# A list scheduler that interleaves two transformer layers: steps chosen by the tile mode of the matrix engine

## The chip, the cores and the metric

The kernel runs on one core of a Trainium2 chip. The core has five engines with an instruction queue each: PE (TensorE, matrix products; its weight loads are listed apart as PEld), ACT (ScalarE, functions such as exp), DVE (VectorE, elementwise and reductions), POOL (GpSimd) and SP (SyncE, here only the issue of DMAs). Products land in PSUM, which has eight banks of 128 x 512 f32. The metric is the device time of one execution in microseconds (us).

## The reference

The input x has 2048 rows of 512 values. Four layers follow each other, A, B, A, B, each adding its output to x after a layer norm; both A layers share their weights, and so do both B layers.

```python
def _A_ref(x, mem0, Wq, Wk, Wv, Wo, seg_len):        # seg_len 32, 8 memory rows, 32 heads of 128
    mem = mem0
    for s in range(n_seg):                            # 64 segments, one after the other
        h = concatenate([mem, x[segment s]])          # 40 rows
        q, k, v = h @ Wq, h @ Wk, h @ Wv              # per head
        p = softmax(where(mask, q @ k.T * scale, -1e9))
        o = (p @ v) @ Wo
        mem = o[:8]                                   # the next segment needs it
        outs.append(o[8:])

def _B_ref(x, wqkv, wo):                              # 32 heads of 16, full attention over 2048 rows
    q, k, v = x @ wqkv
    return softmax(q @ k.T * 0.25) @ v @ wo
```

An A layer is a chain of 64 segments, since each takes its eight memory rows from the one before. A B layer attends from every row to every row without a mask, so its last outputs need the last keys.

## The kernel before, in words

**A segment** is 22 steps on PE, each some 16 to 32 products: Q0 to Q3 and K0 to K3 (projections, `qk_group`, L472), S0 and S1 (scores of 16 heads each, `s_group`, L499, followed by exp on ACT, and mask, sum, reciprocal and scaling on DVE), V0 to V3 (values, `v_round`, L487), T0 and T1 (transposes of the probabilities, `pt_group`, L526), P0 and P1 (probabilities times values, `pv_group`, L538), W0 to W3 (output projection, `wo_part`, L550). The order in which they are considered is a string:

```python
PLAN = "Q0 K0 Q1 K1 S0 Q2 K2 Q3 K3 S1 T0 V0 V1 P0 V2 V3 T1 P1 W0 W1 W2 W3".split()
```

At its end the eight memory rows are copied into the next segment's input (L644).

**Tile modes.** PE can be used as one 128 x 128 array, or split into row or column strips that work side by side. Q, K, W, the B projections and all transposes of 128 x 128 use the whole array (`full`). S, T and V use two column halves of 64 (`col64`), P two row halves (`row64`), the scores of a B unit four row strips of 32 (`S` in the planner's books), the sums of a B unit four column strips of 32 (`PV`).

**A B layer** is cut into runs (one query chunk of up to 512 columns, one group of four heads, some key tiles) and each run into one to four units. A unit is 512 columns of key tile by query (one key tile by 512 queries, or four by 128): `emit_qk` (L388) writes the scores of four heads to three fixed PSUM banks (`b_SX`) and a fourth taken from a pool of four; ACT takes the exp of the three (L390) and then of the fourth (L391); later `pv_mm` (L401) multiplies the probabilities with the values and adds into the one bank `b_oacc`. The last unit of a run closes it: DVE copies the sum out (L706) or adds it to an earlier partial sum that came by DMA (L713), and the partial sum is stored, or, where the run is final, transposed and divided (`finish`, `tq`, L840); when all eight head groups of a tile are done, `out_tile` transposes (L872) and projects it (L881). There are 1040 units in all, 520 for each B layer. As tiles of 128 rows of an A layer become ready (every fourth segment), `tile_done` queues their projections as a chain of steps and adds runs: 32 units after the fourth tile of layer A, then 8, 24, 8, 56 after the next four, 16, 48, 16, 80, then 24, 72, 24, and 112 after the sixteenth. Runs are taken by layer and then by query chunk. The first B layer's units are worked during the first and second A layer, the second's during the second A layer and after it.

**The planner.** PE's order is written by a greedy loop in Python, `step`, that keeps a modelled clock of PE, ACT and DVE (`Clock`; a change of mode is counted with 0.11 us there). At each call it has four candidates with a modelled ready time each: A, the next step of the segment (`a_pick` looks at the first four open ones and takes the first that is ready); U, the scores of the next unit (ready when `b_SX`, a bank and its operands are free, and fewer than three units wait for their sum); V, the sums of up to two waiting units whose probabilities are ready; M, the next function of a chain (projections, `tq`, `out_tile`). Before, the order is: M if ready, V if two are ready or it must be done, U if the segment is behind its quota, A, then U, V, and else whatever is ready first. `quota` gives each segment a number of units: an eighth of the backlog rounded up, more where the second A layer waits for outputs of the first B layer, at most 12. `segment` (L604) loops `while left or done < quota`: it goes on after W3 until the quota is reached. `drain_until` calls `step` without A, between the two A layers and at the end.

The orders of ACT, DVE, POOL and SP follow the order in which this loop emits their instructions. The scratch pool `t` (two buffers of 128 x 512 bf16) holds normed rows, transposed outputs and the working tile of `check`, which tests that softmax sums are in range; the sums of the A layers lie in `smA`, with 16 slots of one segment each, and are tested every sixteenth segment.

## Time and profile before

| what | value |
|---|---|
| median of 2 runs | 3600.22 us (3599.82 to 3600.61) |
| the profiled execution | 3589.69 us |
| span of its instructions | 3587.9 us |
| mean granted clock of PE | 0.917 |
| PE busy (matrix products) | 3112.4 us, 87% |
| PEld busy (weight loads) | 2281.5 us, 64% |
| ACT busy | 2522.1 us, 70% |
| DVE busy | 1594.7 us, 44% |
| POOL busy | 369.9 us, 10% |

In the rows below, times are in us. A row of a timeline has the start, the length, the engine, the line of the kernel, the operation with its tiles, how many instructions are merged in it (`x32`), and in brackets the idle time of the engine just before it with what ended it. The ends of products on PE are modelled, so steps are timed from the start of one to the start of the next. Rows of windows have the window, its length, and busy time with the number of instructions of each engine; then the granted PE clock, the DMA share and GB/s.

### The profile page before, as it was taken

Reading aid. Unit: us, or ns where it says so; the run is one execution under the profiler, and the core shown is the slowest. Engines: PE = TensorE matmul, PEld = TensorE weight load, DVE = VectorE, ACT = ScalarE, POOL = GpSimd, SP = SyncE. Lnnn points to the kernel's source line nnn. Section 1 sums busy time; section 2 is a strip of 40 time slices with the busy share of each in tenths; the row PEclk is TensorE's granted clock in tenths of the full one; section 3 lists DMA queues with packets and bytes.
Section 4 is the critical chain, followed back from the end, with each engine's and each line's share of the span. In section 5 each row is a group of like instructions: output and inputs, shape, how many; then the busy total and the mean of one; then the engine's idle time right before and its main releaser. Section 6 shows DMA issues by size and latency. Waiting matters only on the chain.

```text
span 3587.9 us, 186067 instructions
## 1 busy us (share of the span) xinstructions
PE 3112.4 (87%) x85206; PEld 2281.5 (64%) x85249; DVE 1594.7 (44%) x3887; ACT 2522.1 (70%) x3367; POOL 369.9 (10%) x621
## 2 busy tenths in 40 slices
PE   4999999999998898788899999999998898877555
PEld 3887777776776765455677767777676675543332
DVE  1333434555545454355454544455564554434001
ACT  1444666767778788766876666676867778777886
POOL 0000001111111111101010001111111111000000
PEclk9999999999999998789999999999999999866555
DMA  6001112333334243434332122242334334343441
GB/s 219 16 20 34 38 46 75 98 91 99 112 98 127 82 141 100 122 106 129 97 91 64 42 65 68 78 117 80 112 104 121 109 92 146 101 123 117 122 115 43
DMA packets 318476, 337.25 MB, mean 94 GB/s; under 512 B 93296, under 2 KB 251120, under 8 KB 317680
## 3 DMA queue, kind: packets, MB, share of 16 engines
q1 hardware_dynamic: 279520, 221.67, 22.2%
q0 software_dynamic: 32384, 94.68, 8.2%
q8 instruction: 668, 10.94, 1.3%
q10 hardware_dynamic: 5776, 8.91, 0.8%
q14 instruction: 128, 1.05, 0.1%
HBM read 230.47 MB, written 94.63 MB: 91 GB/s over the span
## 4 chain that ended last, share of the span: by engine, by line
PE 73%; ACT 12%; issue 8%; DVE 4%; DMA 3%; SPq 0%; POOL 0%; ACTq 0%; DVEq 0%; POOLq 0%
PE bank L472 24%; PE bank L550 12%; PE bank L487 11%; ACT b_pt L390 10%; PE b_SX L388 10%; PE b_oacc L401 6%; PE bank L499 2%; PE bank L526 2%; PE bank L791 2%; PE bank L538 1%; DVE a_V L221 1%; PE bank L840 1%; PE bank L812 1%; DMA a_Wv<-in_A_Wv_dram 1%; ACT b_pt L391 1%
## 5 line engine op out<-in xcount | busy, mean ns | idle before, releaser
L390 ACT ACTIVATE b_pt<-b_SX 128x1536 bf16<-128x1536 f32 (+2 forms) x1040 | 1490.8, 1433 | 536.2 <-PE bank L388 487.8
L388 PE MATMUL b_SX<-b_q,b_k 32*128 32x128 bf16 (+1 forms) x6624 | 455.7, 292 | 281.7 <-ACT b_pt L390 269.7
L391 ACT ACTIVATE b_pt<-bank 128x512 bf16<-128x512 f32 (+2 forms) x1040 | 612.8, 589 | 0.5 <-PE bank L388 0.5
L472 PE MATMUL bank<-a_hT,a_Wq 128*128 128x40 bf16 x16384 | 509.7, 182 | 41.2 <-ACT a_QT L219 16.9
L487 PE MATMUL bank<-a_Wv,a_hT 128*64 128x512 bf16 x4096 | 509.7, 383 | 26.0 <-DVE a_V L221 15.6
L472 PEld LDWEIGHTS <-a_Wq 128*128 128x128 bf16 x16384 | 464.5, 97 | 95.3 <-issue 78.8
L472 PE MATMUL bank<-a_hT,a_Wk 128*128 128x40 bf16 x16384 | 506.7, 182 | 8.9 <-issue 4.8
L388 PEld LDWEIGHTS <-b_k 32*128 32x128 bf16 x8832 | 198.7, 99 | 464.2 <-issue 432.9
L550 PE MATMUL bank<-a_OT,a_Wo 128*128 128x40 bf16 x16384 | 475.7, 180 | 14.2 <-DVE a_OT L221 9.0
L472 PEld LDWEIGHTS <-a_Wk 128*128 128x128 bf16 x16384 | 459.7, 97 | 43.8 <-issue 36.4
L550 PEld LDWEIGHTS <-a_Wo 128*128 128x128 bf16 x16384 | 438.3, 96 | 58.0 <-issue 39.7
L401 PE MATMUL b_oacc<-b_pt,b_v 128*17 128x128 bf16 (+2 forms) x8832 | 440.0, 293 | 11.5 <-DVE b_ain L713 3.0
L388 PE MATMUL bank<-b_q,b_k 32*128 32x128 bf16 (+2 forms) x2208 | 445.9, 292 | 2.8 <-DVE b_xo L884 2.5
L487 PEld LDWEIGHTS <-a_hT 128*64 128x64 bf16 x4096 | 219.2, 110 | 195.5 <-issue 59.3
L504 DVE TENSOR_TENSOR a_pn<-a_pn,c_mask 128x256 bf16<-128x256 bf16 x256 | 74.6, 292 | 443.9 <-ACT a_pn L502 443.6
L401 PEld LDWEIGHTS <-b_v 128*17 128x17 bf16 x8832 | 155.3, 94 | 174.9 <-issue 139.6
L221 DVE CAST a_OT<-bank 128x320 bf16<-128x320 f32 x413 | 186.9, 485 | 132.9 <-PE bank L538 131.9
L713 DVE TENSOR_TENSOR b_ain<-b_oacc,b_ain 128x512 f32<-128x512 f32 (+2 forms) x256 | 167.7, 655 | 167.9 <-PE b_oacc L401 159.6
L221 DVE CAST a_QT<-bank 128x320 bf16<-128x320 f32 x259 | 126.8, 490 | 227.8 <-PE bank L472 223.8
L718 POOL DMA_DIRECT2D b_A<-b_aout x208 | 113.7, 547 | 1065.2 <-DVE b_aout L706 1037.0
L219 ACT CAST a_V<-bank 128x512 bf16<-128x512 f32 x292 | 168.9, 597 | 61.4 <-PE bank L487 57.9
L718 POOL DMA_DIRECT2D b_A<-b_ain x176 | 95.6, 543 | 952.8 <-DVE b_ain L713 927.3
(93 smaller groups left out, 2696.7 us busy)
## 6 DMA issues: line engine op xcount, KB each, us to landing
b_ain<-b_A SPq DMA_DIRECT2D x224, 256.0 KB, 2.8
b_A<-b_ain POOLq DMA_DIRECT2D x176, 256.0 KB, 2.6
b_k<-b_K SPq DMA_DIRECT2D x325, 128.0 KB, 2.4
b_q<-b_Q SPq DMA_DIRECT2D x240, 128.0 KB, 2.5
b_v<-b_V SPq DMA_DIRECT2D x448, 68.0 KB, 2.0
b_A<-b_aout POOLq DMA_DIRECT2D x192, 64.0 KB, 2.3
x_after_a<-a_xo POOLq DMA_DIRECT2D x32, 256.0 KB, 3.6
b_Q<-b_qst POOLq DMA_DIRECT2D x32, 256.0 KB, 3.6
```

What stands on the lines that cost most here:

```text
L219: self.nc.scalar.copy(dst, src)
L221: self.nc.vector.tensor_copy(dst, src)
L388: nc.tensor.matmul(out[t][:, j * qw:(j + 1) * qw], lhsT=k[32 * t:32 * t + 32, kj * 128:(kj + 1) * 128], rhs=q[32 * t:32 * t + 32, 0:qw], s ...
L390: nc.scalar.activation(pt[:, 0:3, 0:w], self.SX[:, 0:3, 0:w], ACT.Exp, scale=B_SCALE)
L391: nc.scalar.activation(pt[:, 3, 0:w], y.t[:, 0:w], ACT.Exp, scale=B_SCALE)
L401: self.nc.tensor.matmul(self.oacc[32 * t:32 * t + 17, 0:qw], lhsT=u.v[:, kj, 17 * t:17 * t + 17], rhs=u.p[:, t, j * qw:(j + 1) * qw], star ...
L472: nc.tensor.matmul(ps[:, u, :], lhsT=W[:, ft, h * DH:(h + 1) * DH], rhs=h_s[:, ft, 0:L], start=(n == 0) if ft_major else (ft == 0), stop=( ...
L487: nc.tensor.matmul(b.t[64 * ct:64 * ct + 64, :], lhsT=h_s[:, ft, :], rhs=self.Wv[:, ft, n * 512:(n + 1) * 512], start=(ft == 0), stop=(ft ...
L504: nc.vector.tensor_tensor(self.pn[:, st, :, 0:SEG], self.pn[:, st, :, 0:SEG], self.mask[:], ALU.mult)
L550: self.nc.tensor.matmul(ps[:, ft, :], lhsT=self.Wo[:, h, 128 * ft:128 * ft + 128], rhs=self.OT[:, h, :], start=(h == 0 and ft == 0), stop= ...
L713: nc.vector.tensor_tensor(acc[:, w], k.oacc[:, w], acc[:, w], ALU.add)
L718: nc.gpsimd.dma_start(B.Acc_d[self.qc][self.hg][:, self.qo:self.qo + self.qw], acc[:, w])
```

## The change: what it does

- `a_pick` looks at the first six open steps and prefers a ready one whose mode is that of the last PE step; without one it takes the first ready one.
- `step` gets the mode of the next A step (`ma`) and a number `lead`: how many units the segment is behind its even pace. The new order is: V, if three units wait, or if the last step was a unit's scores and two sums are ready; U, if ready (0.3 us of waiting allowed when `lead` is above 1.5) and `lead` is above 0 where the next A step has another mode than the last step, above 0.7 where it has the same; M, if ready and near `full` work, or if A is not ready, or if 2.5 us overdue; A, with 0.2 us of waiting allowed; then M, U, V.
- `segment` loops `while left`: it ends with W3. What is missing to the quota is carried to the next segment as `debt`, counted up to 3.
- `quota` is a third of the backlog, not an eighth, in the second A layer; the upper limit of 12 stays.
- The output tiles of a run's columns become one chain (a, b, a, b, ...) instead of one chain each.
- `smA` has 4 slots instead of 16 and is tested every fourth segment (64 columns at a time instead of 256); the pool `t` has three buffers instead of two.
- The f32 transposes of `tq` are booked as mode `full`.

```diff
-    def step(self, ra=INF, behind=True, unit=True):
+    def step(self, ra=INF, ma=None, lead=INF, unit=True):
+        mode = self.ck.mode
         now = self.ck.t["PE"] + 0.05
         rm, c = self.chain_next()
         ru = self.unit_at() if unit else INF
-        rv, n, must = self.pv_at()
-        if rm <= now:
+        rv, n = self.pv_at()
+        full = len(self.pending) >= 3
+        if rv <= now and (full or (mode == "S" and n >= 2)):
+            what = "V"
+        elif ru <= now + (0.3 if lead > 1.5 else 0.0) and lead > (0.0 if ma != mode else 0.7):
+            what = "U"
+        elif rm <= now and (mode == "full" or ma == "full" or ra > now or rm < now - 2.5):
             what = "M"
-        elif rv <= now and (n >= 2 or must):
-            what = "V"
-        elif behind and ru <= now:
-            what = "U"
-        elif ra <= now:
+        elif ra <= now + 0.2:
             what = "A"
+        elif rm <= now:
+            what = "M"
         elif ru <= now:
             what = "U"
         elif rv <= now:
...
+    MODE = {"Q": "full", "K": "full", "W": "full", "S": "col64", "T": "col64", "V": "col64", "P": "row64"}
+
     def a_pick(self, left):
         now = self.ck.t["PE"] + 0.05
-        best = (INF, None)
-        for x in left[0:4]:
+        best, first = (INF, None), None
+        for x in left[0:6]:
             t = self.a_ready(x[0], int(x[1]), left)
             if t <= now:
-                return t, x
+                if self.MODE[x[0]] == self.ck.mode:
+                    return t, x
+                first = first or (t, x)
             if t < best[0]:
                 best = (t, x)
-        return best
+        return first or best
 
     def quota(self, A, s):
-        q = -(-self.backlog // 8)
+        q = -(-self.backlog // (8 if A.src is None else 3))
...
-        left, work, done = list(self.PLAN), 0.0, 0
-        while left or done < quota:
-            ra, x = self.a_pick(left) if left else (INF, None)
-            more = done < quota and (self.next or self.cur or self.runs)
-            if not left and not more:
-                break
-            what = self.step(ra, done + 0.5 < quota * (work + 0.4) / total, bool(more))
+        left, work = list(self.PLAN), 0.0
+        done = -min(self.debt, 3.0)
+        while left:
+            ra, x = self.a_pick(left)
+            lead = quota * (work + 0.4) / total - done
+            what = self.step(ra, self.MODE[x[0]], lead, done < quota and bool(self.next or self.cur or self.runs))
...
+        self.debt = quota - done if self.backlog else 0.0
...
-        if s % 16 == 15:
-            self.check(self.smA[:].rearrange("p a b -> p (a b)"), 256)
+        if s % 4 == 3:
+            self.check(self.smA[:].rearrange("p a b -> p (a b)"), 64)
...
-                for c in self.outs:
-                    k.finish_chain(c)
-                self.outs = []
+                k.finish_chain(self.out)
...
-                for q in range(nq):
-                    self.out_tile(run.qc, q0 + q, b.free)
+                self.out = k.chain([f for q in range(nq) for f in self.out_tile(run.qc, q0 + q, b.free)], b.free)
```

## The prediction, made before the result was known

> **What bounds the kernel now.** I read the page first, then the windows by stage, cut where W3 gives way to the next Q0, then the same windows for line 390 alone, whose count is the number of units, then PE's timeline. The page's rows give the span and the price of a unit on ACT:

> ```profile
> span 3587.9 us, 186067 instructions
> ```

> ```profile
> L390 ACT ACTIVATE b_pt<-b_SX 128x1536 bf16<-128x1536 f32 (+2 forms) x1040 | 1490.8, 1433 | 536.2 <-PE bank L388 487.8
> L391 ACT ACTIVATE b_pt<-bank 128x512 bf16<-128x512 f32 (+2 forms) x1040 | 612.8, 589 | 0.5 <-PE bank L388 0.5
> ```

> A unit costs ACT 1.43 + 0.59 = 2.02 us. All engines by stage:

> ```profile
> 332.00:1038.70 706.70, 679.49 (x19784) 521.27 (x19793) 350.71 (x849) 489.91 (x717) 85.39 (x140) 1.00 0.28 80
> 1038.70:1449.20 410.50, 360.56 (x9789) 255.78 (x9788) 202.58 (x457) 330.00 (x386) 49.62 (x86) 0.93 0.39 114
> 1449.20:1684.10 234.90, 185.17 (x4006) 122.29 (x4009) 116.58 (x319) 159.75 (x200) 17.04 (x30) 0.84 0.39 113
> 1684.10:1976.10 292.00, 271.11 (x8828) 214.66 (x8830) 137.60 (x339) 214.37 (x285) 27.32 (x45) 0.98 0.33 89
> 1976.10:2316.30 340.20, 325.06 (x9083) 248.47 (x9088) 161.11 (x391) 224.04 (x347) 29.72 (x47) 0.99 0.22 62
> 2316.30:2691.20 374.90, 353.36 (x10156) 263.36 (x10161) 208.87 (x491) 270.74 (x350) 51.88 (x88) 1.00 0.36 103
> 2691.20:3155.80 464.60, 408.29 (x11166) 293.60 (x11164) 231.50 (x525) 364.19 (x430) 57.64 (x99) 0.93 0.39 114
> 3155.80:3587.90 432.10, 261.15 (x4079) 135.22 (x4081) 87.34 (x255) 339.57 (x367) 29.57 (x53) 0.56 0.37 103
> ```

> The columns after the length are PE, PEld, DVE, ACT, POOL, granted clock. Line 390 alone:

> ```profile
> 332.00:1038.70 706.70, 251.41 (x173) 1.00 0.28 80
> 1038.70:1449.20 410.50, 228.45 (x157) 0.93 0.39 114
> 1449.20:1684.10 234.90, 109.10 (x83) 0.84 0.39 113
> 1684.10:1976.10 292.00, 127.59 (x88) 0.98 0.33 89
> 1976.10:2316.30 340.20, 103.13 (x71) 0.99 0.22 62
> 2316.30:2691.20 374.90, 168.59 (x116) 1.00 0.36 103
> 2691.20:3155.80 464.60, 250.31 (x172) 0.93 0.39 114
> 3155.80:3587.90 432.10, 252.25 (x182) 0.56 0.37 103
> ```

> The stages hold 33, 14, 5, 12, 16, 16 and 16 segments; the last is the tail, with no A work left. Two prices follow. Where PE is the bound (busy 94% and more, clock 0.99 to 1.00), the two middle stages of 16 segments differ by 45 units and 34.7 us: **0.77 us a unit**. In the tail ACT is the bound: 432.1 / 182 = **2.37 us a unit**. The rich stages (1038.7 on, 2691.2 on) lie between: 29.3 us for 11.2 units in a segment. One of them, from 3006.0, shows how:

> ```profile
> 3028.55 1.77 PE L550 MATMUL bank<-a_OT,a_Wo 128*128 128x40 bf16 x64
> 3030.26 0.39 PE L388 MATMUL b_SX<-b_q,b_k 32*128 32x512 bf16 x3
> ...
> 3036.25 0.61 PE L388 MATMUL b_SX<-b_q,b_k 32*128 32x512 bf16 x3 [1.13 <-ACT b_pt L390]
> ...
> 3037.20 1.27 PE L472 MATMUL bank<-a_hT,a_Wq 128*128 128x40 bf16 x32
> ```

> ```profile
> 3006.00:3030.30 24.30, 13.14 (x9) 0.89 0.47 141
> 3030.30:3037.20 6.90, 4.59 (x4) 0.87 0.51 167
> ```

> Its last Wo ends at 3030.3 with nine units done beside the plan in 24.3 us. Then the loop flushes the quota: four units in 6.9 us, 1.7 us each, while the next Q0, which needs none of them, stands behind on PE.

> **The change: fewer mode borders.** A border is priced by a segment without units (the first six rows) and one with many:

> ```profile
> 108.69 0.95 PE L472 MATMUL bank<-a_hT,a_Wk 128*128 128x40 bf16 x32
> 109.49 0.95 PE L472 MATMUL bank<-a_hT,a_Wq 128*128 128x40 bf16 x32
> 110.37 0.43 PE L499 MATMUL bank<-a_KT,a_QT 128*64 128x40 bf16 x15
> ```

> ```profile
> 113.65 0.43 PE L526 MATMUL bank<-c_ident,a_pn 128*64 128x40 bf16 x16
> 113.92 1.03 PE L487 MATMUL bank<-a_Wv,a_hT 128*64 128x512 bf16 x8
> 114.79 0.41 PE L499 MATMUL bank<-a_KT,a_QT 128*64 128x40 bf16 x16
> ```

> ```profile
> 3022.99 0.39 PE L388 MATMUL b_SX<-b_q,b_k 32*128 32x512 bf16 x3
> ...
> 3023.32 0.39 PE L401 MATMUL b_oacc<-b_pt,b_v 128*17 128x512 bf16 x4
> 3023.64 0.37 PE L538 MATMUL bank<-a_PT,a_V 40*128 40x40 bf16 x16
> ```

> K to Q in one mode takes 0.80 us from start to start, Q to S with a change 0.88; T to V, both column halves, 0.27 for 16 products, V to S 0.87. So a border is about 0.09 us; a unit or a sum alone, 0.33, holds one or two. PLAN as written has seven borders; by the new choice Q0 to K3, then S, V and T, then P, then W leave three. Per unit I count half a border less: two sums share one entry behind a unit, but runs of one or three units leave a single last sum, and above a lead of 0.7 units still go into a run of Q or W. With some units standing on the remaining borders, a segment of seven to nine units saves 4 + 4 = 8 borders, 0.7 us, one of three to five about as much. Against it stands that S0 now waits until K3 is over, so that only V covers both softmaxes: 0.2 us of stall a segment, an estimate between none and the rival's 3 us below, near the lower end because V0 to V3 take four of the steps of 0.87 us and further units and P0 can be placed. Net 0.5 us in the stages bound by PE. Segments without units gain five borders (0.45 us) and lose the W0 that stood between T1 and P1: nothing.

> **No flush, carried debt.** What a rich segment holds beside its plan is then the nine units of 24.3 us, less 0.7 for borders. Work of finished tiles adds the difference between the stage's mean and this segment: 24.3 + 2.2 units x 1.7 = 28.0 of 29.3, so 1.3 us. That makes 24.9, taken as 24.8 us with nine units. With a quota of 12 and a debt of 3 the lead stays above 1.5, so a unit goes out as soon as `b_SX` is free; its cover is A's own steps. Where PE waits for it, up to 0.3 us, the next A step stands behind it; nine such waits would be 2.7 us a segment, or 113 us in 42 rich segments. I take none, since the 24.3 us hold such waits already, and keep the bound for the range.

> A unit that moves takes its loads on SP along (a key and a value piece, a query tile, a partial sum) and, where it closes a run, a store on POOL. Both queues keep the order of the units, each load is issued four units ahead, and the DMA share is 0.22 to 0.39 in all stages; I count nothing.

> **Backlog by thirds.** The arrivals in the second A layer are 72 units in the stage from 1976.1, then 136, then 200, and 112 at the end. I carry the backlog along, nine units where it is rich:

> - 332.0: 33 segments x 0.5 = -17 us, still 173 units.
> - 1038.7: 14 x 24.8 = 347, -63; 126 units, 31 fewer.
> - 1449.2: the drain between the layers stays; four segments no longer stop for a flush, which is worth at most 6.9 - 4 x 0.77 = 3.8 us, taken as 2.5: -10.
> - 1684.1: now rich throughout: 12 x 24.8 = 298, +6; 108 units, 20 more.
> - 1976.1: 26 units more x 0.77 = +20, less 16 x 0.5: +12.
> - 2316.3: 15 more, +12 - 8 = +4.
> - 2691.2: 16 x 24.8 = 397, -68; 144 units, 28 fewer.
> - Tail: 178 units, 4 fewer: -9.

> **Small edits.** The 24 additional tests are four DVE instructions each, on shorter rows, beside a DVE that is busy 231.5 of 464.6 us in the fullest rich stage; uncovered they would cost 24 x some 2 us. The third buffer of `t` can only release a writer earlier. The chain a, b, a, b exposes a copy between a and b for each of the last four tiles instead of about one: three more of some 0.6 us (L391 has as many columns) and their handovers, +3. Chains now stand behind units in the tail, which keeps ACT fed there; what it returns I leave at nothing, since a late `tq` holds an accumulator.

> **Sum.** -17 - 63 - 10 + 6 + 12 + 4 - 68 - 9 + 3 = -142 us. The profiled execution took 3589.7 us, of which 1.8 lie outside the span: 3448. The median of the runs shown is 0.3% above it: **3458 us**.

> [...] In the flush rows the idle time of PE is 1.13 us, yet the scores behind it take 0.61 us instead of 0.39, and the rich stages have a clock of 0.93. [...]

> **The rivals.**

> *No change.* What is no longer flushed at 1.7 us ends in the tail at 2.37. In 42 rich segments 2.2 units each, 92 x 0.67 = 62 us, would eat what borders return (65 segments x 0.5 and 42 x 0.7 = 62). It needs the middle stages not to take the 61 units that my ledger gives them, because the planner's books find ACT or banks taken. For it: the tail has the same 112 last units in any case. Against it: ACT is busy 66% and 72% in the two middle stages. About 3600 us; 0.17.

> *Slower: the softmax in the open.* A unit stands on the border between K3 and S0, so its 2.02 us of exp come before S0's exp on ACT's queue; DVE then has two softmaxes in a row. Their length:

> ```profile
> 3020.27 0.29 DVE L504 TENSOR_TENSOR a_pn<-a_pn,c_mask 128x256 bf16<-128x256 bf16 x1 [0.91 <-ACT a_pn L502]
> ...
> 3021.35 0.49 DVE L512 TENSOR_TENSOR a_pn<-a_pn,a_r 128x320 bf16<-128x320 bf16 x1
> ```

> 1.57 us each. Queued behind S0's DVE work are V's evictions, hence banks, hence PE. T1 is ready 2.02 + 0.4 (S0's exp, by L391's 0.59 and its 320 columns) + 3.1 = 5.5 us after the border; two S, four V and T0 give PE some 0.27 x 3 + 0.87 x 4 = 4.3 us and the unit 0.33. One unit costs 1 us a segment, a second unit ahead of S1's exp makes it 3. It decides from 2 us in each of 111 segments with units, (72 + 142) / 111; at 2.2 us the sum is -142 + 244: 3700 us; 0.10.

> *Faster still: the clock.* 0.93 means 14% of the time at half speed, so of the 30 segments at 0.93 some 2 us each, -60; and with ACT fed without gaps a rich segment holds ten units, 42 x (2.37 - 0.77) = -67. 3330 us; 0.13.

> *Borders not saved.* The planner's order follows its own clock, and leads above 0.7 put units into runs as before. Then 33 and 32 segments lose the 0.5 and 42 lose the 0.7: +62, 3520 us; 0.15.

> **Chances.** The forecast has 0.45. A measurement of this kernel tells some 2% from no change, 72 us, so the bounds are 3528 and 3672. Faster: 0.45 + 0.13 and 0.12 of the 0.15 that lie at the bound, 0.70. Slower: 0.10. The rest, 0.20. The range reaches halfway to the clock's case below (3385) and nearly to no change above (3590).

> **What would show it.** In the profile after: P0 and P1 next to each other and S after K3; sums merged as x8 behind a unit; no idle PE of 1.1 us behind the last Wo; stages of nine or more units at about 25 us; a tail of about 178 units. Idle PE in front of T1, V or P would speak for the slower case, a tail above 190 units for no change, a clock of 1.00 in the rich stages for the faster one. Wrong is the prediction if the rich segments keep 29 us, or if the middle stages do not take more units.

## The result and the profile after

| | before | after |
|---|---|---|
| median of 2 runs | 3600.22 us | 3445.33 us (3442.92 to 3447.74) |
| ratio, 95% interval | | 0.957 [0.953, 0.961] |
| profiled execution, its span | 3589.69, 3587.9 us | 3442.92, 3441.1 us |
| mean granted clock | 0.917 | 0.934 |

The kernel is 4.3% faster; 3458 us was predicted, in a range from 3385 to 3590. The total came out 13 us beside the forecast, but several terms of its sum did not. The page of the profile after has these rows:

```profile
span 3441.1 us, 186277 instructions
...
PE 3037.4 (88%) x85249; PEld 2237.6 (65%) x85249; DVE 1572.4 (46%) x3974; ACT 2518.3 (73%) x3376; POOL 369.8 (11%) x621
...
PEclk8999999999999999799999999999999999985655
```

ACT does the same work in 147 us less. The windows of the profile after are cut at the same places as before (columns: window, length, then PE, PEld, DVE, ACT and POOL busy, granted clock, DMA share, GB/s); one stage without units stands in front:

```profile
73.80:326.10 252.30, 239.55 (x7826) 206.92 (x7826) 85.50 (x236) 120.75 (x277) 12.96 (x18) 1.00 0.07 17
326.10:1035.90 709.80, 671.05 (x19792) 520.53 (x19791) 343.49 (x866) 488.91 (x722) 85.50 (x140) 0.99 0.28 79
1035.90:1392.50 356.60, 334.23 (x9700) 242.01 (x9692) 199.10 (x467) 305.29 (x360) 46.90 (x81) 1.00 0.43 123
1392.50:1611.40 218.90, 182.77 (x3848) 116.02 (x3844) 119.95 (x329) 167.09 (x206) 18.33 (x32) 0.88 0.45 129
1611.40:1922.90 311.50, 284.16 (x9224) 220.69 (x9224) 157.48 (x394) 244.98 (x298) 28.58 (x48) 0.99 0.36 94
1922.90:2265.20 342.30, 323.61 (x9516) 251.97 (x9512) 155.96 (x405) 228.00 (x353) 38.89 (x64) 0.99 0.25 70
2265.20:2654.00 388.80, 362.29 (x10700) 271.53 (x10693) 195.12 (x482) 311.44 (x404) 51.24 (x87) 0.99 0.37 104
2654.00:3066.30 412.30, 383.95 (x10810) 276.86 (x10808) 219.48 (x515) 347.24 (x420) 52.88 (x91) 0.98 0.44 125
3066.30:3441.10 374.80, 235.30 (x3349) 114.04 (x3345) 84.65 (x246) 296.00 (x322) 25.73 (x46) 0.57 0.38 105
```

Line 395, which was line 390, alone in the stages that moved most (ACT busy, and in brackets the number of units):

```profile
1035.90:1392.50 356.60, 211.53 (x146) 1.00 0.43 123
...
1922.90:2265.20 342.30, 106.41 (x73) 0.99 0.25 70
...
2654.00:3066.30 412.30, 233.94 (x161) 0.98 0.44 125
3066.30:3441.10 374.80, 219.38 (x159) 0.57 0.38 105
```

Against the stages of before, in order (the first, without units, took 258.6):

| stage (start before) | length before, after | measured | predicted | units before, after (predicted) |
|---|---|---|---|---|
| without units | 258.6, 252.3 | -6 | 0 | none |
| 332.0, bound by PE | 706.7, 709.8 | +3 | -17 | 173, 173 (173) |
| 1038.7, rich | 410.5, 356.6 | -54 | -63 | 157, 146 (126) |
| 1449.2 | 234.9, 218.9 | -16 | -10 | 83, 87 |
| 1684.1 | 292.0, 311.5 | +20 | +6 | 88, 111 (108) |
| 1976.1, bound by PE | 340.2, 342.3 | +2 | +12 | 71, 73 (97) |
| 2316.3 | 374.9, 388.8 | +14 | +4 | 116, 133 (131) |
| 2691.2, rich | 464.6, 412.3 | -52 | -68 | 172, 161 (144) |
| tail | 432.1, 374.8 | -57 | -9, and +3 for small edits | 182, 159 (178) |

Unrounded, the measured column adds up to -147, the predicted one to -142. Two things stand out. The stage that only the mode borders were to shorten did not get shorter. And a rich segment holds 146 / 14 = 10.4 units in 25.5 us, where nine in 24.8 us were expected; what is done there no longer waits in the tail.

A rich segment of the profile after, PE's timeline (start, length, engine, line, tiles, and how many products are merged):

```profile
2941.91 0.39 PE L393 MATMUL b_SX<-b_q,b_k 32*128 32x512 bf16 x3
...
2942.24 0.61 PE L406 MATMUL b_oacc<-b_pt,b_v 128*17 128x512 bf16 x8
2942.78 0.43 PE L504 MATMUL bank<-a_KT,a_QT 128*64 128x40 bf16 x16
...
2959.03 1.77 PE L555 MATMUL bank<-a_OT,a_Wo 128*128 128x40 bf16 x64
2960.74 0.39 PE L393 MATMUL b_SX<-b_q,b_k 32*128 32x512 bf16 x3
...
2961.62 0.96 PE L477 MATMUL bank<-a_hT,a_Wq 128*128 128x40 bf16 x32
```

The pair of sums behind a unit is there (x8), and the next Q0 starts 0.88 us after the scores that follow the last Wo, with no flush between them. But S0 still comes early: after a unit no A step has the mode of the last PE step, so `a_pick` falls back to the order of `PLAN`. In a segment without units S waits for K3, as predicted (the profile after, PE's timeline):

```profile
111.68 0.95 PE L477 MATMUL bank<-a_hT,a_Wk 128*128 128x40 bf16 x32
112.56 0.43 PE L504 MATMUL bank<-a_KT,a_QT 128*64 128x40 bf16 x16
...
117.26 0.37 PE L543 MATMUL bank<-a_PT,a_V 40*128 40x40 bf16 x16
117.99 0.37 PE L543 MATMUL bank<-a_PT,a_V 40*128 40x40 bf16 x16 [0.36 <-DVE a_PT L222]
```

### The profile page after: what moved, and what is told of

It reads as the page before. It is cut to its first block, busy times and chain, and to the rows that moved or that the text cites. A ratio compares the mean times of both kernels' runs of the same rounds, so it can differ in the third digit from the quotient of the medians.

```text
span 3441.1 us, 186277 instructions
## 1 busy us (share of the span) xinstructions
PE 3037.4 (88%) x85249; PEld 2237.6 (65%) x85249; DVE 1572.4 (46%) x3974; ACT 2518.3 (73%) x3376; POOL 369.8 (11%) x621
## 4 chain that ended last, share of the span: by engine, by line
PE 63%; issue 17%; ACT 11%; DVE 5%; DMA 3%; POOL 1%; SPq 0%; POOLq 0%; DVEq 0%; ACTq 0%
PE bank L477 22%; PE bank L555 11%; PE bank L492 9%; ACT b_pt L395 9%; PE b_SX L393 8%; PE b_oacc L406 4%; PE bank L800 1%; PE bank L504 1%; PE bank L531 1%; ACT b_pt L396 1%; PE bank L543 1%; PE bank L821 1%; DMA a_Wv<-in_A_Wv_dram 1%; PE bank L393 1%; DVE a_sm L512 1%
## 5 line engine op out<-in xcount | busy, mean ns | idle before, releaser
L393 PE MATMUL b_SX<-b_q,b_k 32*128 32x128 bf16 (+2 forms) x6624 | 445.2, 284 | 172.0 <-ACT b_pt L395 158.9
L477 PE MATMUL bank<-a_hT,a_Wq 128*128 128x40 bf16 x16384 | 501.6, 180 | 51.0 <-ACT a_QT L220 16.9
L477 PEld LDWEIGHTS <-a_Wq 128*128 128x128 bf16 x16384 | 456.0, 96 | 91.0 <-issue 69.5
L477 PE MATMUL bank<-a_hT,a_Wk 128*128 128x40 bf16 x16384 | 499.6, 180 | 15.5 <-issue 14.1
L555 PE MATMUL bank<-a_OT,a_Wo 128*128 128x40 bf16 x16384 | 460.5, 180 | 12.0 <-ACT a_OT L220 4.5
L406 PE MATMUL b_oacc<-b_pt,b_v 128*17 128x128 bf16 (+2 forms) x8832 | 420.5, 286 | 25.7 <-DVE b_ain L722 10.5
L393 PE MATMUL bank<-b_q,b_k 32*128 32x128 bf16 (+2 forms) x2208 | 435.0, 284 | 5.1 <-DVE a_xo L785 1.9
L220 ACT CAST a_V<-bank 128x512 bf16<-128x512 f32 x377 | 221.8, 599 | 55.5 <-PE bank L492 52.8
L222 DVE CAST a_QT<-bank 128x320 bf16<-128x320 f32 x294 | 144.0, 490 | 159.6 <-PE bank L477 150.9
L222 DVE CAST a_KT<-bank 128x320 bf16<-128x320 f32 x293 | 143.4, 489 | 115.5 <-PE bank L477 95.5
```

What stands on the lines that cost most here:

```text
L220: self.nc.scalar.copy(dst, src)
L222: self.nc.vector.tensor_copy(dst, src)
L393: nc.tensor.matmul(out[t][:, j * qw:(j + 1) * qw], lhsT=k[32 * t:32 * t + 32, kj * 128:(kj + 1) * 128], rhs=q[32 * t:32 * t + 32, 0:qw], s ...
L406: self.nc.tensor.matmul(self.oacc[32 * t:32 * t + 17, 0:qw], lhsT=u.v[:, kj, 17 * t:17 * t + 17], rhs=u.p[:, t, j * qw:(j + 1) * qw], star ...
L477: nc.tensor.matmul(ps[:, u, :], lhsT=W[:, ft, h * DH:(h + 1) * DH], rhs=h_s[:, ft, 0:L], start=(n == 0) if ft_major else (ft == 0), stop=( ...
L555: self.nc.tensor.matmul(ps[:, ft, :], lhsT=self.Wo[:, h, 128 * ft:128 * ft + 128], rhs=self.OT[:, h, :], start=(h == 0 and ft == 0), stop= ...
```

## The experiments

The theory is the prediction's: the gain is the overlap (flush, debt, thirds), with a small part from fewer borders. The rival says that the borders, that is the new order in `step` and `a_pick`, make most of it. All ratios are to the kernel before, run beside the experiment, with a 95% interval.

### The change in halves

The kernel before with the flush taken out and the debt put in:

```diff
-        left, work, done = list(self.PLAN), 0.0, 0
-        while left or done < quota:
+        left, work = list(self.PLAN), 0.0
+        done = -min(self.debt, 3.0)
+        while left:
...
+        self.debt = quota - done if self.backlog else 0.0
```

> The kernel before, with one edit: a segment ends with W3 and carries up to 3 missing units as debt; the order of steps, the steps' choice and the quota by eighths stay. Theory 'overlap' (the gain comes from units that run beside the next segment's A work, and from spreading the backlog; mode borders are worth little): rich segments of about 25.5 us with 9 units, but without thirds the middle stages do not take the rest, so the tail grows to about 205 units: 3555 us. Theory 'borders' (fewer borders make the room for the units): nothing is gained, since units flushed at 1.7 us each end in the tail at 2.37: 3600 us or more.

Measured: 3567.13 us, 0.988 [0.986, 0.990]. The first rich stage went from 410.5 to 348.9 us, but with 124 units in place of 157, and the tail from 182 units to 215, 510.3 us long. The flush stopped PE, yet of the 80 units that leave the stages with a flush (1038.7, 1449.2, 2691.2) 33 end in the tail, and the others lengthen the middle stages: 24.8 us for 18 units in that from 1684.1, 25.8 for 25 in that from 1976.1.

The kernel before with thirds:

```diff
-        q = -(-self.backlog // 8)
+        q = -(-self.backlog // (8 if A.src is None else 3))
```

> The kernel before, with one edit: the quota of the second A layer is a third of the backlog, not an eighth; the flush behind W3 stays. Overlap: a tail of about 130 units, 50 fewer, but the segments that take them flush too: 3560 to 3600 us. Borders: 3600 us.

Measured: 3606.33 us, 0.998 [0.997, 0.999]. The tail has 145 units, but the stages from 1684.1 and 2316.3 grew by 36 and 40 us, for 18 and 16 units more: 2.0 and 2.5 us each, as dear as in the tail, where a hidden one costs 0.77. With the flush, thirds only choose where a unit is dear.

Both together:

> The kernel before, with both edits of the loop and the quota (no flush, debt, thirds), and nothing of the modes: old choice of steps, old order in step. Overlap: the kernel after plus 42 rich segments x 0.7 us for their borders, 3475 us (3450 to 3510). Borders: at least half of the gain is missing, 3525 us or more.

Measured: 3525.15 us, 0.976 [0.975, 0.978]; the theory's 3475 is missed by 50 us. The rest of the change, the order in `step` and `a_pick` without the overlap (the kernel after with flush and eighths, so with the small edits too):

```diff
-        q = -(-self.backlog // (8 if A.src is None else 3))
+        q = -(-self.backlog // 8)
...
-        done = -min(self.debt, 3.0)
-        while left:
+        done = 0.0
+        while left or done < quota:
...
```

> The kernel after, with the flush behind W3 and the quota by eighths put back: the mode rules alone. Overlap: 3570 us (42 rich segments x 0.7 us less than before; nothing in the stages bound by PE). Borders: half of the gain or more, 3525 us or less.

Measured: 3529.51 us, 0.977 [0.975, 0.980], and the theory's 3570 is missed by 40 us. Each half gives some 2.3%, and 0.976 x 0.977 = 0.954 is the whole within its interval. So the order, with the small edits in it, is worth as much as the overlap, and the theory falls there. The small edits (one chain of output tiles, `smA`, the third buffer of `t`) were not run alone. Where does it act? The rich stage, by the windows of the two (columns as above), first the overlap without the order:

```profile
1041.60:1391.20 349.60, 325.69 (x9530) 239.26 (x9527) 195.19 (x442) 269.29 (x325) 44.12 (x76) 1.00 0.40 112
```

and its exps alone (line 391 there):

```profile
1041.60:1391.20 349.60, 180.23 (x124) 1.00 0.40 112
```

then the order without the overlap:

```profile
1037.00:1425.80 388.80, 342.37 (x9790) 244.46 (x9788) 199.25 (x465) 331.72 (x390) 49.52 (x86) 0.98 0.43 122
```

Without the order 124 units take 349.6 us, with both 146 take 356.6: 22 units for 7 us, 0.3 us each. And with the flush kept, the same 157 units as before take 388.8 in place of 410.5.

### Which part of the order

ACT's timeline of the kernel with the overlap alone shows what is missing there:

```profile
1270.87 1.45 ACT L391 ACTIVATE b_pt<-b_SX 128x1536 bf16<-128x1536 f32 x1 [0.63 <-PE bank L389]
...
1276.37 1.45 ACT L391 ACTIVATE b_pt<-b_SX 128x1536 bf16<-128x1536 f32 x1 [0.64 <-PE bank L389]
```

ACT waits 0.6 us for scores, since chains, sums and A steps that are ready go before them; over this rich stage its idle time ahead of the exps of units is 0.59 us a unit. The second theory: a ready unit ahead of everything is what fills the rich segments, not the tile modes. The next kernel is that one with this rule and nothing on modes:

```diff
-        if rm <= now:
+        if rv <= now and len(self.pending) >= 3:
+            what = "V"
+        elif ru <= now + (0.3 if lead > 1.5 else 0.0) and lead > 0.5:
+            what = "U"
+        elif rm <= now:
             what = "M"
...
-        elif behind and ru <= now:
-            what = "U"
...
```

> The kernel before with no flush, debt and thirds (0.976 alone), and in step only this: a sum goes first if three units wait, then a unit that is ready within 0.3 us where the segment is behind, then chains, sums and A as before. No rule on modes anywhere. Unit first: it comes to most of the kernel after, 0.960 to 0.965. Order of A: it stays near 0.976.

Measured: 3464.67 us, 0.961 [0.959, 0.962]. This rule (with the 0.3 us that PE may wait for a unit, and sums first where three wait) takes 1.6 of the 1.9 points between both overlap edits (0.976) and the whole change (0.957). The kernel has none of the small edits, so these and all that the modes do come to 0.4 together. Its rich stage, in the windows, and its exps alone (line 393 there):

```profile
1040.80:1400.60 359.80, 338.85 (x9685) 243.89 (x9681) 201.57 (x456) 299.65 (x354) 46.27 (x80) 1.00 0.42 119
```

```profile
1040.80:1400.60 359.80, 208.74 (x144) 1.00 0.42 119
```

144 units in 359.8 us, nearly what the kernel after does, with ACT idle for 0.40 us ahead of a unit's exps, and with 486 borders there, counted in the trace (before 495, after 441). The 45 borders less in the kernel after are worth 45 x 0.09 = 4 us by the prediction's price, and its stage is 3 us shorter with two units more.

From the kernel after, three parts of the order were taken out singly. The choice by mode in `a_pick`:

```diff
-        for x in left[0:6]:
+        for x in left[0:4]:
...
-                if self.MODE[x[0]] == self.ck.mode:
-                    return t, x
-                first = first or (t, x)
+                return t, x
```

> The kernel after with the old choice of A steps: the first ready one of the first four, without regard to modes; the new order in step stays. Theory 'order of A' (same-mode steps first save the borders that made the room): half of what the mode rules gave, some 40 us, is lost: 0.968 of the time before, rich segments with fewer than 10 units. Theory 'unit first' (what gives the room is that a ready unit now goes out ahead of chains, sums and A steps, and that PE waits up to 0.3 us for it): 0.957 as the kernel after, rich segments of 25.5 us with 10.4 units; in the stages bound by PE more borders and fewer stalls in front of T1, no change in sum.

Measured: 3469.86 us, 0.962 [0.961, 0.964]. The pairing of sums behind a unit:

```diff
-        if rv <= now and (full or (mode == "S" and n >= 2)):
+        if rv <= now and (full or n >= 2 or (n == 1 and self.pending[0].last)):
```

> The kernel after, but sums go as before the change: two ready ones at any place, or the last of a run alone, and not behind a unit only. If pairing saves borders that matter: about half a border a unit, 1040 x 0.5 x 0.09 = 47 us at most, less in the tail, where PE waits anyway: 0.964 to 0.968. If units that go first carry the gain: 0.957 to 0.960.

Measured: 3470.36 us, 0.962 [0.960, 0.963]; the rich stage takes 368.6 us, 12 more, with 147 units. The 0.3 us that PE may wait for a unit:

```diff
-        elif ru <= now + (0.3 if lead > 1.5 else 0.0) and lead > (0.0 if ma != mode else 0.7):
+        elif ru <= now and lead > (0.0 if ma != mode else 0.7):
```

> The kernel after without the 0.3 us that PE may wait for a unit. Unit first: an A step of 0.8 us goes ahead whenever the score banks come free just too late, so ACT starves between units; rich segments fall from 10.4 towards 9 units and the tail grows towards 180: 0.970. Order of A: no change, 0.957.

Measured: 3463.26 us, 0.960 [0.959, 0.962]; the rich stage falls to 132 units, and the tail gets 178. Each of the three is worth 0.3 to 0.5 of a point, less than the theory that needs it expected, and the intervals touch that of the kernel after ([0.953, 0.961]): small, of the expected sign, not settled to the tenth. Last, the kernel after with eighths:

```diff
-        q = -(-self.backlog // (8 if A.src is None else 3))
+        q = -(-self.backlog // 8)
```

> The kernel after with the quota of the second A layer by eighths again; no flush, debt and the mode rules stay. Without thirds e1 had a tail of 215 units where e3 had 181, and lost 0.0115 to it. If spreading the backlog is worth the same beside the new order: 0.957 + 0.012 = 0.969. If units that go out first make it needless: 0.957.

Measured: 3493.75 us, 0.967 [0.965, 0.970]; 192 units are left for the tail. Thirds are worth 1.0 point once units are fed early, and 0.2 alone.

### Where the saved borders went

In the stage from 332.0, the one of 33 segments with few units, PE's changes of mode, counted in the trace, fall from 756 to 612: 144 x 0.09 = 13 us. But the stage is 3 us longer. PE's waits over the whole span (what waited, for what: us, times, longest), first of the kernel before:

```profile
PE b_SX L388 <- ACT b_pt L390: 269.7, 277, 1.6
...
PE bank L472 <- issue: 13.2, 28, 1.6
...
PE bank L526 <- DVE a_pn L512: 1.2, 1, 1.2
```

of the kernel after:

```profile
PE b_SX L393 <- ACT b_pt L395: 158.9, 222, 1.3
...
PE bank L477 <- issue: 30.2, 57, 1.7
...
PE bank L531 <- DVE a_pn L517: 16.2, 24, 1.5
```

and of the one with the old `a_pick` (the choice by mode taken out):

```profile
PE bank L477 <- issue: 32.3, 55, 3.0
...
PE bank L531 <- DVE a_pn L517: 0.9, 1, 0.9
```

T waits for the softmax for 16.2 us, against 1.2; 8.9 of them lie in the stage from 326.1. With the old `a_pick` the wait is gone, and the stage takes 705.4 us, though PE changes its mode 691 times there. This is the rival "the softmax in the open". Its mechanism was a unit in front of S, whose exps stand before S's exp on ACT; so the next kernel is the one after without units there (unless nothing else is ready):

```diff
-    def step(self, ra=INF, ma=None, lead=INF, unit=True):
+    def step(self, ra=INF, ma=None, lead=INF, unit=True, before_s=False):
...
-        elif ru <= now + (0.3 if lead > 1.5 else 0.0) and lead > (0.0 if ma != mode else 0.7):
+        elif ru <= now + (0.3 if lead > 1.5 else 0.0) and lead > (0.0 if ma != mode else 0.7) and not before_s:
...
```

> The kernel after, but no unit is put ahead of its turn where the next A step is S, so that S0's exp does not stand behind a unit's 2.02 us of exp on ACT. If that border unit is what exposes the softmax in the stages bound by PE (idle PE 31.8 us from segment 16 to 48 against 18.9 before), idle PE there falls back to about 19 us and these stages shorten by some 13 us: 0.954. If not, no change: 0.957.

Measured: 3421.77 us, 0.949 [0.948, 0.951]: better than the kernel after, and by more than the 0.954 expected. Its waits:

```profile
PE bank L477 <- issue: 27.9, 54, 1.2
...
PE bank L531 <- DVE a_pn L517: 6.3, 13, 0.8
```

T's wait for the softmax falls by 9.9 us, all waits in front of T by 6.2 (23.5 to 17.3), since more of them end with another engine's work. The span falls by 24.9, 8 of them in segments 16 to 32 and 10 in the stage from 1922.9. Segments 16 to 32, the first with units, by the windows of the kernel after and of this one:

```profile
326.10:668.60 342.50, 323.82 (x9633) 260.29 (x9633) 136.87 (x363) 219.56 (x377) 35.27 (x55) 1.00 0.20 56
```

```profile
325.20:659.20 334.00, 320.45 (x9618) 255.10 (x9618) 151.93 (x381) 209.85 (x358) 34.09 (x54) 1.00 0.20 57
```

The lengths vary: this order has 334.0, 338.9 and 338.6 us there in three kernels (this one and the two below), the order with units in front of S 342.5 to 348.3 in five (the kernel after, with flush and eighths, with eighths, with sums as before, without the 0.3 us). Not all of the price is traced either. In segments 33 to 48 T's wait for the softmax fell from 7.8 to 2.4 us while their length stayed (367.3 and 367.2), and in segments 16 to 32 it was 1.1 in both: there small waits on exps of units went instead (2.0 us to 0.3, and 1.7 to none). So units in front of S cost some 25 us, of which the wait for the softmax can carry 10 at most; how the rest arises isn't shown.

### The clock in the tail

In the tail the granted clock is 0.57, with PE waiting for ACT to free the score banks (112.0 us in 110 waits). The rival "faster still" counts on getting back the clock that the rich stages had lost: 0.93, with pauses of 1.13 us in the flush. The profile after has a pause of this kind in a stage bound by PE: three windows of 3.4 us, and what PE's timeline has in the first of them:

```profile
588.70:592.10 3.40, 1.75 (x70) 1.64 (x67) 0.00 (x0) 0.85 (x2) 0.00 (x0) 1.00 0.06 15
592.10:595.50 3.40, 3.40 (x77) 2.22 (x73) 0.00 (x0) 1.91 (x4) 0.00 (x0) 0.50 0.02 5
595.50:598.90 3.40, 3.40 (x62) 2.06 (x60) 2.39 (x7) 3.03 (x6) 0.56 (x1) 1.00 0.30 100
```

```profile
591.50 0.62 PE L477 MATMUL bank<-a_hT,a_Wk 128*128 128x40 bf16 x18 [1.65 <-issue]
```

One pause of 1.65 us makes PE busy 1.75 of 3.40 us, and the next 3.4 us run at half rate (0.50), full of work. If such pauses do the same in the tail, products that nobody needs should keep it at full rate. The next kernel adds, to the one without units before S, 17 products of 128 columns behind each sum wherever no A work is left; nobody reads what they write:

```diff
-            self.step()
+            if self.step() == "V":
+                self.warm()
+
+    def warm(self):
+        b, at = self.take()
+        for _ in range(17):
+            self.nc.tensor.matmul(b.t[:, 0:128], lhsT=self.ident[:], rhs=self.ident[:], start=True, stop=True)
+        b.free = self.ck.pe(0.95, at, "full")
...
```

> The kernel of e7 (0.9494), and where no A work is left (between the layers and in the tail) PE gets 17 additional products of 128 columns behind each sum, some 0.95 us, whose result nobody reads. Theory 'busy share' (the clock of the next 3.4 us follows the busy share of PE in this one): the tail keeps the full clock, scores take 0.33 instead of 0.53 us, ACT loses its 0.28 us between units, and 158 units at 2.0 instead of 2.3 us make some 30 to 40 us: 0.940. Theory 'idle time' (only a long gap of PE slows it): the clock in the tail stays at 0.57, the products last twice as long and hold up the scores: 0.950 or more.

Measured: 3430.87 us, 0.952 [0.950, 0.954]; the 0.940 of the theory "busy share" is missed, and the time is the one that "idle time" gave. The windows of its drain between the layers and of its tail:

```profile
1386.20:1482.40 96.20, 87.27 (x1663) 61.91 (x1662) 37.95 (x112) 74.57 (x92) 10.80 (x18) 0.95 0.48 133
3060.60:3429.80 369.20, 327.50 (x6007) 238.73 (x6012) 82.79 (x244) 297.13 (x324) 25.74 (x46) 0.97 0.39 108
```

But the clock is 0.97, as "busy share" had it, and not 0.57. Still the tail is only 6 us shorter than without (375.1), and the drain is 17 longer (78.8). PE's and ACT's timelines, where output tiles are due, show why:

```profile
3300.49 1.12 PE L459 MATMUL bank<-c_ident 128*128 128x128 bf16 x17
```

```profile
3302.05 1.45 ACT L395 ACTIVATE b_pt<-b_SX 128x1536 bf16<-128x1536 f32 x1 [0.98 <-PE bank L393]
```

The block takes 1.1 us and stands in front of an output tile and the next scores; ACT then waits 0.98 us for these. So the last kernel has the products only in the tail, and only where no chain falls due within 1.0 us:

```diff
-            if self.step() == "V":
+            if self.step() == "V" and self.tail and self.chain_next()[0] > self.ck.t["PE"] + 1.0:
                 self.warm()
...
```

> The kernel of e7 (0.9494) with the additional products of e11, but only in the last drain, and only where no chain falls due within the next 1.0 us. In e11 they kept the clock but stood in front of output tiles, and made the drain between the layers 17.5 us longer. Without these two costs a unit of the tail takes 2.0 us where nothing else is due: a tail of about 340 us instead of 367, 0.942. If the units' own wait for ACT is what sets the tail, whatever the clock: 0.949.

Measured: 3405.85 us, 0.943 [0.941, 0.945], 1.4 points below the kernel of the change (0.957): better than both kernels. The tail is 20 us shorter than without the products (375.1), where some 27 were expected. Its tail in the windows, and on ACT:

```profile
3051.60:3407.20 355.60, 313.28 (x5653) 220.29 (x5655) 84.42 (x246) 295.92 (x322) 25.80 (x46) 0.97 0.41 112
```

```profile
3199.74 1.45 ACT L396 ACTIVATE b_pt<-b_SX 128x1536 bf16<-128x1536 f32 x1 [0.37 <-PE bank L394]
3201.09 0.59 ACT L397 ACTIVATE b_pt<-bank 128x512 bf16<-128x512 f32 x1
3201.75 1.45 ACT L396 ACTIVATE b_pt<-b_SX 128x1536 bf16<-128x1536 f32 x1
```

In the tail of the kernel after, ACT has these rows:

```profile
3215.91 1.45 ACT L395 ACTIVATE b_pt<-b_SX 128x1536 bf16<-128x1536 f32 x1 [0.28 <-PE bank L393]
...
3218.12 1.45 ACT L395 ACTIVATE b_pt<-b_SX 128x1536 bf16<-128x1536 f32 x1 [0.27 <-PE bank L393]
```

With the products three units in four take at most 2.05 us, ACT's own 1.43 + 0.59, where in the tail of before and after most took 2.21, with a wait of 0.27 us for scores at half rate (0.54 us from start to start at 3197.5 in after, at a clock of 0.50, against 0.33 at 2941.9, at 1.00). On average over the tail it is 2.12 us against 2.23, which is 17 of the 20 us.

## Why the prediction was right, and where it was not

**The total** is right, in part by luck: it comes through terms that were wrong on both sides. Against their terms the stage from 332.0 took 20 us more, the rich ones 9 and 16, those from 1684.1 and 2316.3 14 and 10; the tail with the small edits took 51 less, the stage from 1976.1 10, that from 1449.2 and the segments without units 6 each. That is 68 us too much against 73 too little. The other 8 us of the 13 come from the step to the median, which lay 10 us above the profiled execution before, and 2 after.

**"Fewer mode borders", 8 a segment and 0.5 us net: this step failed.** The price held: in segments without units 69 borders less (126 to 57) shorten 15 segments by 6.3 us, 0.09 us each, which the step put at nothing because of the displaced W0. But the count did not: 144 / 33 = 4.4 borders saved a segment (54 / 14 = 3.9 in the first rich stage), since a unit resets the mode and `a_pick` then follows `PLAN`. That is 13 us. T's wait took 7.7 us of it, close to the 0.2 us a segment that the step had set aside. What it had nothing for: waits that the profile puts down to "issue", 10.1 us in the stage over all lines where there were 5.4, and half rate behind the pauses, 17.1 us of the stage by its clock records where there were 3.4, some 7 us of work.

**No flush: right in direction, mis-sized.** The 24.8 us with nine units of the step are 25.5 us with 10.4. The step took its nine from a segment of before, where chains, sums and A steps went ahead of a unit, and credited the steady feed to the missing flush ("so a unit goes out as soon as `b_SX` is free"). The overlap edits without the order show 124 / 14 = 8.9 units in 25.0 us: the step's figure is that kernel's. The 1.5 units more come from the new order of `step`, which the prediction had costed by borders alone: with a unit ahead of what is ready, and no rule on modes, it was 144 / 14 = 10.3.

**The ledger of units** shifted with that. The two rich stages hold 146 and 161 units, not 126 and 144, and the stage from 1976.1 gets 73, not 97, because its backlog had been worked off. The tail has 159, not 178; at 2.37 us these 19 are 45 of the 51 us. Rich segments and the tail were the two ends of one error.

**The tail's price** stayed: 374.8 / 159 = 2.36 us. That chains stand behind units there shows no return in this price, as taken.

**The rivals.** *No change* needed the middle stages to refuse units; two of the three took 23 and 17 more. *The softmax in the open* is there, at a tenth of its price at most: the wait for the softmax is 16 us, and units in front of S cost 25 in all, not 244; its own condition, 2 us in each segment, is never near, since T waits 24 times in all. *Borders not saved*: half true of the stage bound by PE. *Faster still* was right in both its conditions, ten units and a clock of 1.00 in the rich stage (0.98 in the other), but the 2 us a segment that it booked for the clock show in no rich stage: the forecast's 24.8 us for nine units, with 0.77 for each further one, gives 25.9 and 25.6, and 25.5 and 25.8 were measured. Its ten units came as a shorter tail. The lower bound of the range, called halfway to this case, lies 9 us beyond it: halfway is 3394. The sum counts nothing for the clock: that filled pauses return none was the author's estimate, and beyond the rich stages no run shows it. Behind a window with 1.65 us of pause the clock of after was 0.50 for 3.4 us, and products that nobody reads raised 0.58 to 0.97 in the tail, where they were worth 20 us.

**What stays open.** The wait that ends with "issue" in front of Q and K products grew from 13.2 to 30.2 us. It is 27.3 in the kernel with the overlap alone and 32.3 with the old `a_pick`, so the long runs of one mode don't make it; what does wasn't found.

## What to carry to other kernels

Where two engines share a stage, ask first which of them the greedy order lets run dry: here one rule, the unit that feeds ACT ahead of nearly everything that is ready, was worth 1.6%, and the tile modes and small edits beside it 0.4 together. Spreading work over more segments pays only where its price there is the hidden one (thirds: 0.2 points beside a flush, 1.0 without). A step that is moved to save a border, 0.09 us here, should be checked for what then stands in front of its successor on another engine's queue.
